# An attention and gated-FFN kernel on one core: halves of matmul pairs dealt as 6, 6 and 12 steps, places planned over the whole loop, one score of long cycles copied by ScalarE

## The chip, the cores and the metric

One Trainium2 chip, one of its cores. A core has TensorE (PE; its weight loads are listed apart as PEld), VectorE (DVE), ScalarE (ACT), GpSimd (POOL) and SyncE (SP, which here issues all DMAs). Each engine runs its own instructions in order and they meet through semaphores. PSUM has eight banks of 128 x 512 fp32 values; TensorE writes them, VectorE and ScalarE read them. The metric is the device time of one execution in microseconds (us).

## The reference: what is computed

```python
# x: 2048 tokens of width 512, all fp32
xn = layernorm(x)
# 32 heads of width 16, all tokens attend to all tokens
q, k, v = split_heads(xn @ wqkv)
p = softmax(q @ k.T * 16**-0.5)
s = merge_heads(p @ v) @ wo
# bilinear gated FFN, width 1792
f = ((xn @ w_gate) * (xn @ w_up)) @ w_down
out = x + s * silu(f)
```

## The kernel before, in words

**Units, rounds, blocks, cycles.** Heads are taken four at a time (8 groups) and queries 512 at a time (4 chunks): 32 units. A unit has 16 rounds, one for each tile of 128 keys; a round has four *positions*, one for each head. So there are 2048 positions. Position q does two things. `expo` computes t, the scores of 128 keys by 512 queries, on TensorE (line 668), and e = exp(t) on ScalarE (line 670) from one of three PSUM banks ("st"). `score` computes, 86 positions ahead of its use (`LEAD`), the scores s of 128 queries by 512 keys (line 646); VectorE reduces them to their maximum (line 648) from one of three other banks ("s"). The maxima of a unit are joined in `maxima`, go through DRAM, and come back as two extra rows of the queries, so that t arrives with the maximum subtracted. t and s of a position use different halves of TensorE's rows and run side by side.

Two rounds, eight positions, make a *block*: `block` multiplies their e with V (pv, line 685; 16 records), into a bank of "st". ScalarE copies the result out (line 698, into one of two single `part` tiles) and GpSimd adds it to the unit's sum. The loop has 256 *cycles*, one for each block: some positions, then the block's pv.

**Filler.** Between the positions of a cycle stand *steps* of other matmuls: the projections of q and k, then the FFN's gate, up and down products, then the output projection. Every fp32 product is made as three products of split operands (high and low part) with 64 rows each, so two sums, a *pair*, run at once on the two halves of TensorE's rows. A pair is made in two halves, because each sum has to pass over both row halves; `pair` (line 283) swaps them in the middle. At the swap a tiny ScalarE activation called `look` (line 304) reads one value of the pair, and the second half's first matmul waits for it. A half has 12 steps, or 15 in the down products of the first two thirds of the FFN. When a pair is done, ScalarE copies one sum and VectorE deals with the other: a copy (line 337), a product (line 387) or an addition (line 462), queued in `before_values` and issued after the cycle's last position, in front of pv.

**What sets the order.** The program's order on TensorE, ScalarE, VectorE and GpSimd is the order in which Python issues it. Three choices set it.

- How many cycles a pair gets, and how its steps fall on them: `spread` and `Filler.fetch`. 240 cycles are shared out in proportion to steps; a pair gets two, three or four. With an odd number, the middle cycle holds the end of the first half and the beginning of the second.
- How many positions a cycle gets: `fits`, seven to nine by its steps, held between one and four positions (`AHEAD`) beyond what the cycle's block needs.
- Where steps stand within a cycle: `Filler.spread` and `Filler.part`, evenly over the gaps between positions; none stands before the second position or after the last but one.

```python
fits = min(9, max(7, int(2.6 + 0.62 * work))) if q + LEAD < TOTAL and work else 8
```

In words below, (p,w) is a cycle of p positions and w steps; (7,4+3) has the swap inside.

**Before the loop.** `early` normalizes the tokens, projects the first keys, queries and all of V, and computes the first 86 scores; a table, `EARLY`, says at which of 265 steps how many scores stand. Each chunk of 512 keys goes through DRAM (`KD`) before scores can use it. **After the FFN**, `ending` projects the output, over the last cycles and beyond the loop.

Of the kernel before, what the change touches and what calls it, by code (L numbers as in the profile page):

```python
# [13 lines left out]
AF = mybir.ActivationFunctionType  # L14
# [16 lines left out]
THIRDS = [range(0, 5), range(5, 10), range(10, 14)]  # L31
LEAD = 86
CYCLES = 240
AHEAD = range(1, 5)
SLOTS = 24 * (NC * (NG // 2 - 1) + 1) + 36 * NF * NC
SPLIT_ROUNDS = 3
EBUFS = 11
HBUFS = 2
QBUFS = 2
EARLY = {66: 4, 75: 4, 84: 4, 93: 4, 104: 4, 113: 4, 124: 6, 137: 4, 144: 2, 150: 2, 156: 4, 162: 2, 166: 2,  # L40
         170: 2, 175: 2, 180: 4, 186: 2, **{n + m: k for n in (192, 216, 240) for m, k in ((0, 2), (6, 2), (12, 4), (18, 2))}}
EARLY_BUFS = {"s": 4, "x": 2, "f": 2}
BUFS = {"st": 3, "s": 3, "misc": 2}
LOWER, UPPER = slice(0, 64), slice(64, P)
BEHIND = mybir.DependencyInfo(mybir.DependencyClass.Sync, mybir.DependencyReason.DATA)
ORDER = mybir.DependencyInfo(mybir.DependencyClass.NoSync, mybir.DependencyReason.SCHED_ONLY)
ORDERED = {mybir.EngineType.PE, mybir.EngineType.Activation, mybir.EngineType.DVE, mybir.EngineType.Pool}


def body(ctx, tc, x, wqkv, wo, wg, wu, wd, out):  # L50
# [87 lines left out]
        while waiting and waiting[0][0] <= steps[0]:  # L138
            waiting.pop(0)[1]()

    before_values, behind_values, lighter = [], [], [False]

    def run_all(queue):
        while queue:
# [489 lines left out]
            for pr in range(2):  # L634
                dma(k[b:b + 2, pr].bitcast(F32), ones)

    def score(n, other, tag="s"):

        i, r = divmod(n, 4 * NT)
        r, j = divmod(r, 4)  # L640
        j ^= other
        kc, t = divmod(r, 4)
        b, pr = 64 * (j % 2), j // 2
        k = ks[(i // NC) % 2]
        o = psum(tag, f"s{i}_{r}_{j}")
        nc.tensor.matmul(o, QS[i][b:b + KB, pr, t * P:(t + 1) * P],  # L646
                         k[b:b + KB, pr, kc * 512:(kc + 1) * 512], start=True, stop=True)
        nc.vector.tensor_reduce(MX[i][:, j, t, kc:kc + 1], o, axis=AX.X, op=OP.max)  # L648

    def maxima(i):  # L650
        mm = keep.tile([P, 3, 4, 4], F32R, name="mm", bufs=2)
# [99 lines left out]
    def early():  # L751
# [76 lines left out]
        def v(*tts):  # L828
            for tt in tts:
                yield from v_proj(wv, tt, "f")  # L830

        at = {n: [] for n in range(265)}
        for c, stats, apply, turns in ((1, (0, 2, 4, 6), (25, 25, 25, 25), (38, 42, 46, 50)),
                                       (2, (26, 26, 28, 30), (60, 60, 73, 75), (70, 74, 79, 83)),
# [4 lines left out]
        for tts, n, root, scale in ((tuple(range(4, 8)), 0, 13, 16), (tuple(range(8, NT)), 16, 52, 53)):  # L839
# [4 lines left out]
        at[150].append((exp_table, None))  # L844
        at[205].append((ahead, 1))
        at[130] += [(ones_columns, slice(8, NT)), (other_keys, None)]
        gens = [k(0), q(0), v(0, 1, 2), k(1), q(1), v(3), k(2), v(4, 5), k(3),
                *[v_pair(wv, (tt, tt + 1), "xf"[tt // 2 % 2]) for tt in range(6, NT, 2)]]
        scored = 0
        stream = (n for g in gens for n in g if n == 1)  # L850
# [45 lines left out]
    class Filler:  # L896
# [4 lines left out]
            self.left, self.queue, self.done = 0, [], False  # L901
            self.plan = []

        def share(self, n, gaps):

            return [n * (i + 1) // gaps - n * i // gaps for i in range(gaps)][::-1]
# [26 lines left out]
        def spread(self, gaps):  # L933
            if isinstance(self.now, tuple):
                a, b = self.now
                self.plan = self.share(a, 2) + [0] + self.share(b, gaps - 3)
            else:
                self.plan = self.share(self.now, gaps)

        def part(self):  # L940
            n = self.plan.pop(0) if self.plan else 0
# [4 lines left out]
                if not self.left:  # L946
                    self.fetch()

    cum = [0]

    def spread(n):
        a = cum[0]
        cum[0] += n
        return max(1, round(cum[0] * CYCLES / SLOTS) - round(a * CYCLES / SLOTS))

    def values(rounds, done):
        if before_values:
            run_all(before_values)
        elif not done:
            step_small(heads)  # L960
        run_all(reduced)
        block(rounds)
        run_all(behind_values)
        if rounds[-1][1] == NT - 1:
            heads.append(finish(rounds[0][0]))
            step_small(heads)
# [9 lines left out]
        lighter[0] = False  # L976
        return True

    def position(q):
# [12 lines left out]
        if j == 3 and kt % 4 == 2:  # L992
            gates.append(lambda: step_small(later))
        ready[n][2].append(expo(i, kt, j))
        scored = q + LEAD
        if scored < TOTAL:
            score(scored, 1)
# [7 lines left out]

    with tc.manual_schedule(engines=ORDERED):
        with banks_of(EARLY_BUFS):
            fil = Filler(filler(early()), spread)
        ctx.enter_context(banks_of(BUFS))
        q = 0  # L1010
        for b in range(NU * NT // 2):
            if fil.done:
                parts = iter([3, 2, 2, 2, 2, 2, 2, 2])
                fil = Filler(ending(), lambda n: next(parts))
# [56 lines left out]
```

## Time and profile before

| | |
|---|---|
| median of 3 runs | 1701.24 us (1701.0 to 1701.58) |
| the profiled execution | 1701.59 us |
| its span, first to last instruction | 1699.8 us |
| granted TensorE clock, mean | 0.999 |
| busy: PE, PEld | 1690.4 us (99%), 1042.1 us (61%) |
| busy: DVE, ACT, POOL | 1436.6 us (85%), 1308.2 us (77%), 875.9 us (52%) |
| DMA | 145.94 MB, mean 86 GB/s |

In rows of groups stand line, engine, operation, the tiles written and read (out<-in), shape, count, then busy us, mean ns of one, idle time before them and what ended it. In rows of the timeline stand start and length in us, engine, line, operation, tiles, shape, count, and in brackets the idle time before the row with what ended it. The end of a matmul is modelled, so its start is the better mark. Rows of the chain of waits have start, length and name.

### The profile page before, as it was taken

To read this page: it belongs to the slowest core of one execution; us is meant where nothing else is said; L and a number is where in the kernel's file an instruction comes from. 1 tells how busy PE (TensorE), PEld (TensorE's weight loads), DVE (VectorE), ACT (ScalarE), POOL (GpSimd) and SP (SyncE) were. 2 spreads that over 40 slices of the span, in tenths; PEclk is the share of its full clock that TensorE was granted. 3 is DMA by queue.
4 is the path that set the end of the run, shared out by engine and by line. 5 is a ranking of instruction groups with operands and counts; after the bars stand their busy time and mean duration, and the time that the engine had idled before them with its cause. 6 is when DMAs were issued, how large, how long until landed. Compare 5 with 4: busy or idle time off the path is not lost.

```text
span 1699.8 us, 35273 instructions
## 1 busy us (share of the span) xinstructions
PE 1690.4 (99%) x13702; PEld 1042.1 (61%) x13702; DVE 1436.6 (85%) x2485; ACT 1308.2 (77%) x2573; POOL 875.9 (52%) x877
## 2 busy tenths in 40 slices
PE   9999999999999999999999999999999999999998
PEld 6766566666565666655656665656666566665665
DVE  7888888888888898888888888888888888898952
ACT  6368777778777788777877887877778777787774
POOL 5125545753645648456354672663647536455661
PEclk9999999999999999999999999999999999999999
DMA  6218623520241312412115220330225112111362
GB/s 228 80 60 251 222 110 128 139 61 29 61 86 41 116 42 79 79 48 62 29 53 133 72 68 23 87 77 27 59 81 127 55 36 65 35 48 47 114 187 90
DMA packets 117507, 145.94 MB, mean 86 GB/s; under 512 B 12700, under 2 KB 74396, under 8 KB 114652
## 3 DMA queue, kind: packets, MB, share of 16 engines
q1 hardware_dynamic: 117340, 143.69, 29.2%
q8 instruction: 108, 1.77, 0.4%
q14 instruction: 59, 0.48, 0.1%
HBM read 95.94 MB, written 47.45 MB: 84 GB/s over the span
## 4 chain that ended last, share of the span: by engine, by line
PE 97%; issue 1%; DMA 1%; POOL 0%; ACT 0%; DVE 0%; SPq 0%; DVEq 0%; ACTq 0%; POOLq 0%
PE pv L685 27%; PE t L668 19%; PE s L646 12%; PE y L296 6%; PE u L296 5%; PE g L296 5%; PE g L300 4%; PE u L300 4%; PE y L300 4%; PE p L296 3%; PE z L296 2%; PE p L300 2%; PE last L685 1%; PE v L300 1%; PE v L296 1%
## 5 line engine op out<-in xcount | busy, mean ns | idle before, releaser
L648 DVE TENSOR_REDUCE mx<-s 128x1 f32<-128x512 f32 x2048 | 1256.6, 683 | 206.6 <-PE s L646 166.2
L670 ACT ACTIVATE e<-t 128x512 f32<-128x512 f32 x2048 | 1099.8, 601 | 94.0 <-PE pv L685 40.0
L668 PE MATMUL t<-qs,ks 50*128 50x512 f32 x2048 | 782.9, 407 | 0.0
L646 PE MATMUL s<-ks,qs 48*128 48x512 f32 x2048 | 769.4, 408 | 0.7 <-DMA ks<-KD 0.5
L64 POOL TENSOR_TENSOR acc<-acc,part 128x512 f32<-128x512 f32 x214 | 280.1, 1309 | 556.7 <-ACT part L698 556.5
L668 PEld LDWEIGHTS t<-qs,ks 50*128 50x128 f32 x2048 | 359.3, 185 | 266.7 <-issue 109.8
L685 PE MATMUL pv<-e,V 128*32 128x512 f32 x3968 | 477.1, 598 | 0.0
L646 PEld LDWEIGHTS s<-ks,qs 48*128 48x128 f32 x2048 | 353.2, 185 | 25.9 <-issue 2.8
L698 ACT ACTIVATE part<-pv 128x512 f32<-128x512 f32 x214 | 128.1, 599 | 204.7 <-PE pv L685 202.3
L685 PEld LDWEIGHTS pv<-e,V 128*32 128x32 f32 x3968 | 103.6, 109 | 234.8 <-issue 214.6
L300 PE MATMUL g<-fh,w1h 64*128 64x512 f32 x224 | 90.5, 404 | 0.0
L296 PE MATMUL u<-fh,w0h 64*128 64x512 f32 x224 | 90.4, 404 | 0.0
L296 PE MATMUL y<-dh,hh 64*128 64x512 f32 x224 | 89.1, 398 | 0.0
L300 PE MATMUL y<-dh,hh 64*128 64x512 f32 x224 | 89.0, 398 | 0.0
L300 PE MATMUL u<-fh,w0l 64*128 64x512 f32 x224 | 88.2, 394 | 0.0
L300 PE MATMUL g<-fl,w1h 64*128 64x512 f32 x224 | 88.1, 393 | 0.0
L300 PE MATMUL g<-fh,w1l 64*128 64x512 f32 x224 | 88.0, 393 | 0.0
L296 PE MATMUL g<-fl,w1h 64*128 64x512 f32 x224 | 88.0, 393 | 0.0
L296 PE MATMUL u<-fh,w0l 64*128 64x512 f32 x224 | 88.0, 393 | 0.0
L296 PE MATMUL g<-fh,w1h 64*128 64x512 f32 x224 | 87.9, 392 | 0.0
L300 PE MATMUL u<-fl,w0h 64*128 64x512 f32 x224 | 87.8, 392 | 0.0
L300 PE MATMUL y<-dh,hl 64*128 64x512 f32 x224 | 87.8, 392 | 0.0
(295 smaller groups left out, 3063.7 us busy)
## 6 DMA issues: line engine op xcount, KB each, us to landing
w1r<-in_wg_dram SPq DMA_DIRECT2D x56, 256.0 KB
w0r<-in_wu_dram SPq DMA_DIRECT2D x56, 256.0 KB
wdr<-in_wd_dram SPq DMA_DIRECT2D x56, 256.0 KB
qs<-QD SPq DMA_DIRECT2D x64, 192.0 KB
ks<-KD SPq DMA_DIRECT2D x12, 768.0 KB
KD<-hl SPq DMA_DIRECT2D x16, 512.0 KB
QD<-hl SPq DMA_DIRECT2D x16, 512.0 KB
OD<-acc SPq DMA_DIRECT2D x31, 256.0 KB
```

Source lines behind the costliest of these rows:

```text
L64: got = getattr(self.engine, name)(*args, **kw)
L296: nc.tensor.matmul(outs[k], l[LOWER], r[LOWER], start=k == 0 and n == 0, stop=(stop or k == 0) and n == len(low) - 1, skip_group_check=k == 1)
L300: nc.tensor.matmul(outs[1 - k], l[UPPER], r[UPPER], start=k == 0 and m == 0, stop=(stop or k == 0) and m == len(high) - 1, skip_group_chec ...
L646: nc.tensor.matmul(o, QS[i][b:b + KB, pr, t * P:(t + 1) * P], k[b:b + KB, pr, kc * 512:(kc + 1) * 512], start=True, stop=True)
L648: nc.vector.tensor_reduce(MX[i][:, j, t, kc:kc + 1], o, axis=AX.X, op=OP.max)
L668: nc.tensor.matmul(o, k[b:b + KR, pr, kt * P:(kt + 1) * P], QS[i][b:b + KR, pr], start=True, stop=True)
L670: nc.scalar.activation(e, o, AF.Exp, scale=DH ** -0.5)
L685: nc.tensor.matmul(o[32 * j:32 * j + 32, c], V[:, kt, h0:h0 + 32], es[j][:, c], start=(kt if whole else n) == 0, stop=kt == NT - 1 if whol ...
L698: nc.scalar.activation(part, o, AF.Copy)
```

## The change

Five things, in the order of the diff.

1. *Dealing of pairs.* Every pair, whatever its steps, counts alike in the sharing of the 240 cycles: of 93 pairs 54 get three cycles and 39 two. The first half of a pair with three cycles is spread over two of them and the second half has the third: 6, 6, 12 steps, or 8, 7, 15. No cycle holds a swap.
2. *Places.* A function `plan` chooses the number of positions of every cycle ahead of the loop, by dynamic programming over how many positions stand ahead (now 0 to 4), with a cost for each cycle from two straight lines (`wait`). It gives 6 positions to cycles of 6 steps, mostly 9 or 10 to those of 12, and 12 to eleven of them. In the last cycles none stands ahead.
3. *A copied score.* In cycles of over 10 steps, from the 29th on, where the plan's formula has it cheaper, the score of one position (the seventh in cycles of 12 steps) is copied by ScalarE into a `part` tile, and VectorE reduces the copy later, when the cycle's last position is issued and the pairs' results are dealt with (`held`). 25 cycles have it.
4. *The first cycle* has 12 positions as before, with 6 steps in place of 12 and none in its first gap.
5. *Before the loop*, the projection of the fourth chunk of keys moves eight steps ahead, in between the steps of a V tile, and `EARLY` asks for some scores a few steps later, two of them at step 262 in place of steps 137 and 144.

```diff
-AHEAD = range(1, 5)
-SLOTS = 24 * (NC * (NG // 2 - 1) + 1) + 36 * NF * NC
+HALVES = [3 * ND] * (NC * (NG // 2 - 1) + 1) + NC * [3 * n for third in THIRDS for n in [ND] * len(third) + [len(third)] * 2]
+PROJECTIONS = 2 * (NC * (NG // 2 - 1) + 1)
+LAST = [3, 2, 2, 2, 2, 2, 2, 2]
+AHEAD = range(0, 5)
...
-EARLY = {66: 4, 75: 4, 84: 4, 93: 4, 104: 4, 113: 4, 124: 6, 137: 4, 144: 2, 150: 2, 156: 4, 162: 2, 166: 2,
-         170: 2, 175: 2, 180: 4, 186: 2, **{n + m: k for n in (192, 216, 240) for m, k in ((0, 2), (6, 2), (12, 4), (18, 2))}}
+EARLY = {66: 4, 75: 4, 84: 4, 93: 4, 104: 4, 113: 4, 124: 6, 144: 4, 150: 2, 156: 4, 162: 2, 167: 2, 172: 2, 176: 2,
+         180: 4, 186: 2, 262: 2, **{n + m: k for n in (192, 216, 240) for m, k in ((0, 2), (6, 2), (12, 4), (18, 2))}}
...
+def cycles_of(k):
+    if k >= len(HALVES):
+        return LAST[k - len(HALVES)]
+    a, b = [round(m * CYCLES / len(HALVES)) for m in (k, k + 1)]
+    return max(1, b - a)
+
+def shares(n, gaps):
+    return [n * (i + 1) // gaps - n * i // gaps for i in range(gaps)][::-1]
+
+def parts_of(n, cycles):
+    if cycles == 1:
+        return [(n, n)]
+    return shares(n, (cycles + 1) // 2) + shares(n, cycles // 2)
+
+def room(work):
+    return 2.36 + 0.603 * work
+
+def wait(places, work, copied):
+    slow = 0.3775 * (places - room(work))
+    full = 0.2575 * places - 0.2275 * work - 0.22
+    return max(0, slow, full), max(0, slow - 0.6, full + 0.4) if copied and work > 10 else 9
+
+def plan():
+    work = [sum(w) if isinstance(w, tuple) else w
+            for k, n in enumerate(HALVES + [3 * ND] * len(LAST)) for w in parts_of(n, cycles_of(k))]
+    states, blocks = {AHEAD[-1]: (0, [8 + AHEAD[-1]])}, NG * NC * NT // 2
+    for b in range(1, blocks - 1):
+        new = {}
+        for ahead, (cost, places) in states.items():
+            for later in AHEAD:
+                n = 8 + later - ahead
+                c = cost + 0.003 * (n - 8) ** 2
+                if 8 * b + LEAD < NG * NC * NT * 4:
+                    c += min(wait(n, work[b], b > PROJECTIONS + 1)) + 0.001 * (n - room(work[b])) ** 2
+                if later not in new or c < new[later][0]:
+                    new[later] = c, places + [n]
+        states = new
+    ahead, (_, places) = min(states.items(), key=lambda s: s[1][0])
+    return places + [8 - ahead]
...
-    def score(n, other, tag="s"):
+    def score(n, other, tag="s", copied=False):
...
-        nc.vector.tensor_reduce(MX[i][:, j, t, kc:kc + 1], o, axis=AX.X, op=OP.max)
+        if copied:
+            kept = part_tile()
+            nc.scalar.activation(kept, o, AF.Copy)
+            held.append(lambda: nc.vector.tensor_reduce(MX[i][:, j, t, kc:kc + 1], kept, axis=AX.X, op=OP.max))
+        else:
+            nc.vector.tensor_reduce(MX[i][:, j, t, kc:kc + 1], o, axis=AX.X, op=OP.max)
...
-        gens = [k(0), q(0), v(0, 1, 2), k(1), q(1), v(3), k(2), v(4, 5), k(3),
+        gens = [k(0), q(0), v(0, 1, 2), k(1), q(1), v(3), k(2), v(4), *between(v(5), 4, k(3)),
...
-                    self.whole, odd = divmod(self.cycles(2 * n), 2)
-                    self.split = max(2, round(n / (2 * self.whole + 1))) if odd else 0
-                    self.more = max(2, self.split - 1) if odd and self.whole else n if odd else 0
-                    self.queue = self.share(n - self.split, self.whole) if self.whole else []
-                    if odd:
-                        self.queue.append((self.split, self.more))
-                    if self.whole:
-                        self.queue += self.share(n - self.more, self.whole)
+                    self.queue = parts_of(n, self.cycles())
...
         elif not done:
             step_small(heads)
+        run_all(held)
         run_all(reduced)
...
-            if b >= NU * NT // 2 - 2:
-                last = TOTAL - 4 * (NU * NT // 2 - 1 - b)
-            else:
-                fits = min(9, max(7, int(2.6 + 0.62 * work))) if q + LEAD < TOTAL and work else 8
-                need = 8 * (b + 1)
-                last = min(max(q + fits, need + AHEAD[0]), need + AHEAD[-1], TOTAL - 4) if b else need + AHEAD[-1]
-            count = last - q
             fil.spread(max(2, count - 2))
...
+            elif b == 0:
+                fil.plan = [0] + shares(work, count - 3)
+            plain, copied = wait(count, work, b > PROJECTIONS + 1 and q + LEAD < TOTAL)
+            unit = (q + count + LEAD) // (4 * NT) > (q + LEAD) // (4 * NT)
+            kept = int(room(work)) - 3 if copied < plain and not unit else -1
             for k in range(count):
...
-                position(q)
+                position(q, k == kept)
```

More of the change, by code (lines that the diff above doesn't have):

```diff
@@ L139, in step @@
             waiting.pop(0)[1]()
-    before_values, behind_values, lighter = [], [], [False]
+    before_values, behind_values, held, lighter = [], [], [], [False]
     def run_all(queue):
@@ L830, in v, with between @@
                 yield from v_proj(wv, tt, "f")
+        def between(outer, n, inner):
+            outer = iter(outer)
+            return [(next(outer) for _ in range(n)), inner, outer]
         at = {n: [] for n in range(265)}
@@ L902, in __init__ @@
             self.plan = []
-        def share(self, n, gaps):
-            return [n * (i + 1) // gaps - n * i // gaps for i in range(gaps)][::-1]
         def fetch(self):
@@ L935, in spread @@
                 a, b = self.now
-                self.plan = self.share(a, 2) + [0] + self.share(b, gaps - 3)
+                self.plan = shares(a, (gaps - 1) // 2) + [0] + shares(b, gaps // 2)
             else:
-                self.plan = self.share(self.now, gaps)
+                self.plan = shares(self.now, gaps)
         def part(self):
@@ L947, in part, with cycles @@
                     self.fetch()
[L949 to L954, printed above, removed]
+    pairs = [0]
+    def cycles():
+        pairs[0] += 1
+        return cycles_of(pairs[0] - 1)
     def values(rounds, done):
@@ L977, in two_finished, with position @@
         return True
-    def position(q):
+    def position(q, copied):
         n, j = divmod(q, 4)
@@ L996, in position @@
         if scored < TOTAL:
-            score(scored, 1)
+            score(scored, 1, copied=copied)
         step()
@@ L1007, in body @@
         with banks_of(EARLY_BUFS):
-            fil = Filler(filler(early()), spread)
+            fil = Filler(filler(early()), cycles)
         ctx.enter_context(banks_of(BUFS))
         q = 0
-        for b in range(NU * NT // 2):
+        for b, count in enumerate(plan()):
             if fil.done:
-                parts = iter([3, 2, 2, 2, 2, 2, 2, 2])
-                fil = Filler(ending(), lambda n: next(parts))
+                fil = Filler(ending(), cycles)
             work = fil.begin()
-            if b >= NU * NT // 2 - 2:
-                last = TOTAL - 4 * (NU * NT // 2 - 1 - b)
-            else:
-                fits = min(9, max(7, int(2.6 + 0.62 * work))) if q + LEAD < TOTAL and work else 8
-                need = 8 * (b + 1)
-                last = min(max(q + fits, need + AHEAD[0]), need + AHEAD[-1], TOTAL - 4) if b else need + AHEAD[-1]
-            count = last - q
             fil.spread(max(2, count - 2))
```

## The prediction

> **What bounds the kernel now.** I read the page first, then the chain of waits in order of time, then single engines' timelines.
>
> ```profile
> span 1699.8 us, 35273 instructions
> PE 97%; issue 1%; DMA 1%; POOL 0%; ACT 0%; DVE 0%; SPq 0%; DVEq 0%; ACTq 0%; POOLq 0%
> L670 ACT ACTIVATE e<-t 128x512 f32<-128x512 f32 x2048 | 1099.8, 601 | 94.0 <-PE pv L685 40.0
> ```
>
> TensorE carries 97% of the chain; other engines show in it only where they make TensorE pause. So I take the loop cycle by cycle: from one block of value products (pv, 16 records) to the next. In the chain each block is a row: start, length, name.
>
> ```profile
> 493.98 1.85 PE pv L685 x16
> 500.07 1.85 PE pv L685 x16
> ...
> 849.86 1.85 PE pv L685 x16
> 855.43 1.86 PE pv L685 x16
> 860.99 1.85 PE pv L685 x16
> 867.04 1.85 PE pv L685 x16
> 874.01 1.85 PE pv L685 x16
> ...
> 1005.22 1.85 PE pv L685 x16
> 1011.95 1.85 PE pv L685 x16
> ...
> 1035.15 1.86 PE pv L685 x16
> 1041.15 0.98 PE pv L685 x5
> ```
>
> I write (p,w) for a cycle of p positions and w steps. The cycles from 849.86 on are (7,8), (7,4+3), (8,9) and (9,12): 5.57, 5.56, 6.05 and 6.97 us. (9,12) has 6 slots (positions and steps together) more than (7,8) and takes 1.40 us more: 0.233 a slot. TensorE alone thus needs 2.07 + 0.233(p+w): 6.73 for (8,12), which the cycle at 1005.22 has, and 6.03 for (8,9). Two kinds exceed it. (7,4+3), where a pair changes halves inside the cycle, should take 5.33 and loses 0.23. (8,7), at 1035.15, should take 5.57, takes 6.00 and loses 0.43. The other kind with a change inside, (8,5+4) at 493.98, takes 6.09 against 6.03 and loses about 0.05.
>
> The first loss is a wait for ScalarE. Three rows of the tile "look" (who waited for it: us, times), then TensorE, ScalarE and a weight load in the cycle at 855.43:
>
> ```profile
>   PEld u L296: 5.8, 25
>   PEld y L296: 3.8, 17
>   PEld p L296: 1.4, 6
> ...
> 859.21 0.40 PE L668 MATMUL t<-qs,ks 50*128 50x512 f32 x1
> 859.35 0.14 ACT L304 ACTIVATE look<-u 1x1 f32<-1x1 f32 x1
> 859.55 0.18 PEld L296 LDWEIGHTS u<-fh,w0h 64*128 64x128 f32 x1 [0.23 <-ACT look L304]
> 859.89 0.40 PE L296 MATMUL u<-fl,w0h 64*128 64x512 f32 x1
> ```
>
> The second half's first step starts 0.34 behind t instead of 0.233, and the next 0.34 behind that: 0.21 in all. Where the halves part at a cycle's end, as in (9,12), nothing is lost.
>
> The second loss is VectorE's pace. Two rows of the cycle at 1035.15 and one of ScalarE from 860.61:
>
> ```profile
> 1037.50 4.28 DVE L648 TENSOR_REDUCE mx<-s 128x1 f32<-128x512 f32 x7 [1.27 <-PE s L646]
> 1037.66 3.53 ACT L670 ACTIVATE e<-t 128x512 f32<-128x512 f32 x7
> ...
> 860.61 1.08 ACT L670 ACTIVATE e<-t 128x512 f32<-128x512 f32 x2
> ```
>
> Reductions run end to end, 4.28/7 = 0.61 each, and with three score banks a score waits for the reduction three before it. A position more costs VectorE 0.61 and TensorE 0.233, difference 0.38; a step more lengthens TensorE's side alone by 0.233. From (8,7), the wait is 0.43 + 0.38(p-8) - 0.233(w-7), nothing where negative. It gives nothing for (9,12) and (7,8), as seen.
>
> **The change part by part.** The counts are the two dealing rules and the planner's rule worked through.
>
> *Waits removed.* Before, 36 pairs hold 8, 4+3 and 9 steps, 13 pairs of fifteens hold 10, 5+4 and 11, and three pairs hold 8, 7, 8, 7. Afterwards every change of halves falls on a cycle's end. Saved: 36 x 0.23 = 8.3; 13 x 0.05 = 0.7; three (8,7), 1.3; three (7,7), 0.05 each by the formula, 0.2; and 0.02 (6.05 against 6.03) in 36 (8,9), 0.7: together 11.2 us.
>
> *New cycles.* Between the first cycle and the end come 87 (6,6), 9 (6,7), 10 (7,8), 73 (9,12), 25 (10,12), 22 with 15 steps, 11 (12,12), 2 (7,6) and two single ones. By the formula (6,6) has -0.10, so no wait, with only 0.10 in hand; (6,7), (7,8), (9,12) and the fifteens none; (10,12) 0.03; (7,6) 0.28, twice: 0.6; (12,12) without a copy 0.79, twice: 1.6.
>
> *The copied score.* It stands in 16 (10,12) and 9 (12,12). One reduction of 0.61 leaves the run that TensorE waits for and comes after the last position, in front of the 1.27 in which VectorE was idle; that idle time hides it, and without it the next cycle's scores would be 0.61 late. So 0.18 of the 0.79 is left on that side. ScalarE gets a copy for it. No row shows one from a score bank; the nearest is the exponential, 0.601 long, two in 1.08, so 0.48 apart, and I take that. The first exponential starts 2.51 behind pv (1037.66 against 1035.15); with the copy among them the ninth starts 9 x 0.48 later, at 6.83, and ends at 7.43. The twelfth t, due at 7.33 (7.66, less 0.33 from the last position to pv), needs its bank, and pv the tenth's, 0.48 later: some 0.1 to 0.2 late each. I take 0.34 a cycle, 9 x 0.34 = 3.1, with 0.18 and 0.79 (the copy frees nothing) as bounds. In (10,12) pv needs the eighth's bank, at 6.95 for a start at 7.20; the copy waits for its score, though, which comes late there, and I take 0.08: with the nine uncopied 1.6 (bounds 0 and 25 x 0.15, some two copies' lateness). Sum of new waits: 0.6 + 1.6 + 3.1 + 1.6 = 6.9.
>
> The Trainium skill has a rule that speaks against the copy: "ScalarE: Activation LUTs", section "What ACT_TABLE_LOAD costs", gives an ACTIVATE with immediate scale 186 ns and 0.833 ns an element, less about 93 ns of overlap back to back, an estimate of 0.52 apart for 512. The trace has 0.48. By the Trainium skill's spacing the nine cycles would pay some 0.5 each more, and the sum below would come out 4.5 higher.
>
> *No position ahead.* Before, each block of pv had at least one position of the next block ahead of it. Afterwards 54 loop cycles, all of 6 or 7 steps, and the whole end have none, so pv's second round needs the exponential just issued. At the kernel's end the parts are seen singly:
>
> ```profile
> 1682.22 0.19 PEld L668 LDWEIGHTS t<-qs,ks 50*128 50x128 f32 x2 [0.84 <-ACT e L670]
> 1682.76 2.07 ACT L670 ACTIVATE e<-t 128x512 f32<-128x512 f32 x4 [0.65 <-PE t L668]
> 1685.31 0.39 PE L296 MATMUL z<-fh,w0l 64*128 64x512 f32 x1
> 1685.68 0.16 PEld L685 LDWEIGHTS last<-e,V 128*32 128x32 f32 x8 [0.35 <-issue]
> 1686.56 0.56 PEld L685 LDWEIGHTS last<-e,V 128*32 128x32 f32 x12 [0.30 <-issue]
> ```
>
> The second round starts 0.88 behind the first. An exponential starts 0.54 behind its t and lasts 0.60; the t stands about 0.35 ahead of pv; so it ends 0.79 into pv, hidden with 0.09 in hand. In these cycles the look (0.14, its row above) can stand ahead of it. I take 0.01 each, 0.5; bounds 0 and 54 x 0.14 = 7.6. Behind it on ScalarE stand pv's part copy and the next exponentials, which begin only when pv has ended.
>
> *The start.* Two places ahead of the loop stall:
>
> ```profile
> 47.44 0.73 PE L646 MATMUL s<-ks,qs 48*128 48x512 f32 x4
> 48.10 0.50 PE L276 MATMUL v<-e,xh 128*128 128x512 f32 x1
> ...
> 55.39 0.72 PE L646 MATMUL s<-ks,qs 48*128 48x512 f32 x3
> 56.37 0.46 PE L646 MATMUL s<-ks,qs 48*128 48x512 f32 x1 [0.26 <-DMA ks<-KD]
> 56.76 0.50 PE L276 MATMUL p<-xh,w1l 128*128 128x512 f32 x1
> ...
> 67.34 0.39 PE L300 MATMUL v<-e,xh 64*128 64x512 f32 x1
> 67.90 0.47 PE L646 MATMUL s<-ks,qs 48*128 48x512 f32 x1 [0.18 <-DVE mx L648]
> 68.59 0.47 PE L646 MATMUL s<-ks,qs 48*128 48x512 f32 x1 [0.22 <-DMA ks<-KD]
> 68.91 0.39 PE L300 MATMUL v<-e,xh 64*128 64x512 f32 x1
> ...
> 90.90 3.68 DVE L648 TENSOR_REDUCE mx<-s 128x1 f32<-128x512 f32 x6 [0.30 <-PE s L646]
> 95.17 7.27 DVE L648 TENSOR_REDUCE mx<-s 128x1 f32<-128x512 f32 x12
> ```
>
> Four scores usually take 0.66 (47.44 to 48.10) and took 1.37 from 55.39 on: 0.71 lost to keys not landed. From 67.34 two slots (0.47) took 1.57: 1.10 lost, to the fourth keys and to VectorE. The change asks for those keys later and makes the fourth eight steps sooner, its store and loads on SP's queue with it: of 1.81 I take 1.5 (bounds 0 and 1.8). But two scores move to just ahead of the loop, where VectorE runs without a break from 90.90 to the first pv: 2 x 0.61 = 1.2 later (bounds 0 and 1.2). In the first cycle, paced by VectorE, six steps that it hid move to cycles paced by TensorE: 6 x 0.233 = 1.4.
>
> *The end.* Four positions move from the loop (4 x 0.233 = 0.9 saved) behind the last steps. There the fourth's exponential starts 0.54 + 3 x 0.48 behind the first t, ends 0.60 later, at 2.58, and the second round (half of 1.86) ends at 3.5; now pv, 1.85 long from 1685.68, ends 2.0 behind that point (1685.31 and a slot: 1685.54). So 1.5 - 0.9 = 0.6 (bounds 0 and 1.5).
>
> The sum: -11.2 + 6.9 + 0.5 - 1.5 + 1.2 + 1.4 + 0.6 = -2.1. The profiled execution took 1701.59, 1.8 of it outside its span, and gives 1699.5; the median of the runs shown, 1701.24, is 0.35 lower: 1699.1.
>
> **The rivals.** *The long cycles cost almost nothing.* Every copied (12,12) at 0.18, (10,12) at 0, no late exponential, the start's 1.8 whole: new waits 1.6 + 1.6 + 0.6 = 3.8, and -11.2 + 3.8 - 1.8 + 1.2 + 1.4 + 0.6 = -6.0: 1695.2. For it: the (9,12) rows show none of either wait. Against: ScalarE's count above. *The last exponential ends too late.* At 0.14 in 54 cycles the 0.5 becomes 7.6: +5.0, 1706.2, slower. It decides from about 0.11 a cycle on. For it: 0.09 in hand is less than one look. Against: where VectorE paces, t comes later but pv does too. *The copy frees nothing.* ScalarE, with one operation more, is late by what VectorE gained, and the nine copied (12,12) pay the 0.79: 9 x 0.45 = 4.1 more, 1703.2. The rule on ScalarE's spacing above points this way; the 0.48 points against it. *The look still waits.* The change moves it and doesn't remove it. If the first step of a second half still paid 0.21 in the 54 pairs of three cycles, 11.3 more: 1710.4. That the token itself must stay, the Trainium skill says: "PSUM — Partial Sum Buffer", section "PSUM bank collisions raise a hardware error", has it that row tiles mustn't use one bank at once and that software must order them. Against it: the (9,12) rows.
>
> **How the numbers follow.** The forecast has 0.45, cheap long cycles 0.30, the late exponential 0.14, the copy that frees nothing 0.08, the look 0.03. 0.2% is 3.4 us, about what a measurement of this kernel can tell from no change: faster is below 1697.8, slower above 1704.6. Faster gets the 0.30 and 0.10 of the forecast's lower side; slower gets 0.03 and 0.11 of the late exponential; the rest is the same. The range goes from below the cheap rival to just under the late exponential, 1693.5 to 1705.
>
> **What would show it.** The waits for look in the loop fall from 48 to a few, and (6,6) cycles take 4.87 with pv blocks 4.87 apart. (12,12) cycles take 8.0, (10,12) 7.2 to 7.3. The first pv stands within 0.5 of where it stood. If pv waits for an exponential in the cycles of 6 steps, or they take over 4.95, the forecast is wrong upward; if (12,12) takes 7.7 to 7.85, downward.

## The result and the profile after

The changed kernel takes 1710.24 us (median of 6 runs, 1709.19 to 1710.58); the kernel before, in the same rounds, 1701.38 (1701.0 to 1701.94). The ratio is 1.0052, 95% interval 1.0042 to 1.0063: slower by 8.9 us, where 2.1 us less was forecast, and above the range that ended at 1705. The profiled execution took 1710.56.

From the page of the changed kernel: the span and the chain by engines.

```profile
span 1708.5 us, 35368 instructions
PE 91%; POOL 3%; DMA 2%; DVE 2%; issue 1%; ACT 1%; SPq 0%; DVEq 0%; POOLq 0%; ACTq 0%
```

TensorE's share of the chain fell from 97% to 91%, and GpSimd and DMA, which had 0% and 1%, now carry 3% and 2%: parts of the chain that run past TensorE. The ordinary cycles come out as forecast. These are block starts in the chain of waits of the changed kernel:

```profile
896.15 1.85 PE pv L744 x16
904.23 1.92 PE pv L744 x16
909.16 1.85 PE pv L744 x16
914.01 1.85 PE pv L744 x16
920.97 1.85 PE pv L744 x16
927.91 1.85 PE pv L744 x16
935.12 1.93 PE pv L744 x16
```

A copied (12,12) takes 8.08, the second (6,6) after it 4.85, two (9,12) 6.96 and 6.94, a (10,12) 7.21. (In the chain the block that ends a long cycle stands some 0.07 early, with a row of 1.92 or 1.93 instead of 1.85; from pv's first record to the next the (12,12) takes 8.14 and the (6,6) behind it 4.87.) So I took every cycle of both traces from the first record of one pv to that of the next, and subtracted 2.07 + 0.233(p+w), with 1.40/6 for 0.233. A wait inside a pv thus counts in the cycle behind it. Cycles are numbered from 0 here: cycle 0 is the first, and the 243rd pv ends cycle 242. What is left, in us:

| | before | after |
|---|---|---|
| start of the span to first pv | 101.12 | 100.46 |
| first pv to 243rd pv | 1507.49 | 1514.72 |
| of it waits, by that formula | 9.4 | 15.7 |
| 243rd pv to the end | 91.2 | 93.3 |
| waits by kind, before | (7,4+3) and (7,7) 7.7, (8,7) 1.2, (8,9) and (8,5+4) 0.9 | |
| waits by kind, after | | (12,12) 6.8, (9,12) 5.9, (10,12) 1.5, (6,6) 1.3, (7,6) 0.6, (8,12) 0.4 |

The kinds of after don't lie evenly. 83 of 87 (6,6) and 68 of 73 (9,12) wait for less than 0.1; the 5.9 sits in five (9,12) cycles, and two of these, cycles 4 and 12, have 1.02 and 3.78. (The others are cycle 20 with 0.69, which waits for a `part` tile, and cycles 92 and 144 with 0.42 and 0.45, whose wait lies in the pv ahead of them.) In cycles 4 and 12 TensorE waits for something that it didn't wait for in the kernel before. Cycle 4, from TensorE's timeline:

```profile
126.14 0.47 PE L700 MATMUL s<-ks,qs 48*128 48x512 f32 x1 [0.56 <-DMA qs<-QD]
```

The first pair has three cycles where it had two, so its query projection is stored a cycle later (on SP's queue from 118.06 on instead of 113.84) and the score stands at a query that hasn't landed. Cycle 12, from the chain of waits:

```profile
150.53 10.01 DMA ks<-KD
160.54 0.02 issue
160.56 7.49 DMA QD<-hl
...
168.85 1.29 POOL hl L118
170.14 0.58 POOL tr L118
170.72 1.23 POOL acc L118
171.96 0.02 issue
171.98 0.61 ACT part L757
172.59 0.04 issue
172.63 0.54 PE t L727
173.17 0.42 PE p L350
173.60 0.42 PE p L350
```

Read from below: t waits because ScalarE copies pv's result only at 171.98, into a `part` tile that GpSimd frees at 170.72 plus 1.23; GpSimd was busy splitting a projection into `hl`, whose two buffers were still being stored to DRAM; and those stores stood on SP's queue behind eight loads of the second group's keys. GpSimd's and TensorE's timelines have the two waits:

```profile
165.81 0.61 POOL L118 CAST hl<-qr 128x512 fp32r<-128x512 f32 x1 [3.96 <-DMA KD<-hl]
```

```profile
172.63 0.54 PE L727 MATMUL t<-qs,ks 50*128 50x512 f32 x1 [1.97 <-ACT part L757]
```

SP's timeline shows the order, in the kernel before and then in the changed kernel:

```profile
144.92 0.97 SPq L64 DMA_DIRECT2D KD<-hl  x2
146.85 1.42 SPq L64 DMA_DIRECT2D QD<-hl  x2
148.32 7.24 SPq L64 DMA_DIRECT2D ks<-KD  x8
```

```profile
147.70 8.58 SPq L118 DMA_DIRECT2D ks<-KD  x8
157.37 1.39 SPq L118 DMA_DIRECT2D KD<-hl  x2
159.36 1.51 SPq L118 DMA_DIRECT2D QD<-hl  x2
```

These stores are the third pair's. The first five pairs end in cycles 1, 4, 6, 9 and 11 in the kernel before and in cycles 2, 4, 7, 9 and 12 in the changed one, so the third pair's projection is split from 147.71 on instead of 142.90, while the loads are asked for at almost the same time. The wait is 1.97, the cycle loses 3.78. The last rows of the chain show the rest: after the pause steps are 0.43 apart instead of 0.233. The last section has the clock.

The end grew too. The last cycle's timeline on ScalarE, TensorE and the weight loads:

```profile
1688.04 1.92 PE L744 MATMUL last<-e,V 128*32 128x512 f32 x16
...
1690.48 2.07 ACT L729 ACTIVATE e<-t 128x512 f32<-128x512 f32 x4 [1.74 <-PE t L727]
...
1693.64 2.06 ACT L729 ACTIVATE e<-t 128x512 f32<-128x512 f32 x4
1694.29 0.50 PE L727 MATMUL t<-qs,ks 50*128 50x512 f32 x1 [0.46 <-ACT e L729]
1694.72 2.09 PE L744 MATMUL last<-e,V 128*32 128x512 f32 x24
```

The last block begins 6.68 after the one before it, against 5.31 (1680.37 to 1685.68) in the kernel before: ScalarE has eight exponentials in this cycle instead of four.

### The profile page after: what moved, and what is told of

It is laid out like the page before. It is cut to its first block, busy times and chain, and to the rows that moved or that the text cites. A ratio compares the mean times of both kernels' runs of the same rounds, so it can differ in the third digit from the quotient of the medians.

```text
span 1708.5 us, 35368 instructions
## 1 busy us (share of the span) xinstructions
PE 1694.5 (99%) x13702; PEld 1059.9 (62%) x13702; DVE 1446.2 (85%) x2479; ACT 1312.6 (77%) x2602; POOL 882.0 (52%) x883
## 4 chain that ended last, share of the span: by engine, by line
PE 91%; POOL 3%; DMA 2%; DVE 2%; issue 1%; ACT 1%; SPq 0%; DVEq 0%; POOLq 0%; ACTq 0%
PE pv L744 25%; PE t L727 18%; PE s L700 11%; PE y L350 5%; PE u L350 5%; PE g L350 5%; PE g L354 4%; PE y L354 4%; PE u L354 4%; PE z L350 2%; PE p L350 2%; PE p L354 1%; DVE mx L707 1%; PE last L744 1%; PE z L354 1%
## 5 line engine op out<-in xcount | busy, mean ns | idle before, releaser
L727 PE MATMUL t<-qs,ks 50*128 50x512 f32 x2048 | 790.9, 408 | 3.4 <-ACT part L757 2.9
L700 PE MATMUL s<-ks,qs 48*128 48x512 f32 x2048 | 784.9, 411 | 1.9 <-DVE mx L707 1.2
L744 PEld LDWEIGHTS pv<-e,V 128*32 128x32 f32 x3968 | 108.6, 109 | 227.9 <-issue 174.1
L350 PE MATMUL g<-fh,w1l 64*128 64x512 f32 x224 | 88.0, 393 | 0.0
L354 PE MATMUL g<-fl,w1h 64*128 64x512 f32 x224 | 87.9, 393 | 0.0
L354 PE MATMUL g<-fh,w1l 64*128 64x512 f32 x224 | 87.9, 393 | 0.0
L354 PE MATMUL u<-fh,w0h 64*128 64x512 f32 x224 | 87.9, 393 | 0.0
L350 PE MATMUL u<-fl,w0h 64*128 64x512 f32 x224 | 87.9, 392 | 0.0
L354 PE MATMUL u<-fl,w0h 64*128 64x512 f32 x224 | 87.9, 392 | 0.0
L350 PE MATMUL u<-fh,w0h 64*128 64x512 f32 x224 | 87.9, 392 | 0.0
```

Source lines behind the costliest of these rows:

```text
L350: nc.tensor.matmul(outs[k], l[LOWER], r[LOWER], start=k == 0 and n == 0, stop=(stop or k == 0) and n == len(low) - 1, skip_group_check=k == 1)
L354: nc.tensor.matmul(outs[1 - k], l[UPPER], r[UPPER], start=k == 0 and m == 0, stop=(stop or k == 0) and m == len(high) - 1, skip_group_chec ...
L727: nc.tensor.matmul(o, k[b:b + KR, pr, kt * P:(kt + 1) * P], QS[i][b:b + KR, pr], start=True, stop=True)
L744: nc.tensor.matmul(o[32 * j:32 * j + 32, c], V[:, kt, h0:h0 + 32], es[j][:, c], start=(kt if whole else n) == 0, stop=kt == NT - 1 if whol ...
```

## The experiments

My theory after the two traces: the cycles of the loop are about even, as much lost to VectorE in long cycles as was gained at the swaps, and the 8.9 us come from local accidents (the pile-up at cycle 12, the wait in cycle 4, the end). The rival: the cycles themselves cost more, through the copy or through cycles with no position ahead. The kernel before, measured with each group of runs, had medians of 1700.85, 1700.54 and 1701.17, and 1701.38 in the rounds of the result. They drift by up to 0.8, so what a run gives back is told as its distance from the kernel before of its own rounds, against the changed kernel's 8.9.

### The keys loaded later

```diff
-            if kt == 0 and g + 1 < NG and c == 1:
+            if kt == (6 if g == 0 else 0) and g + 1 < NG and c == 1:
                 load_k(g + 1)
```

> The changed kernel, but the loads of the second group's keys (8 DMAs of 192 KB) are issued six rounds later; nothing else differs. Theory 'pile-up': in the changed kernel these loads stand on SP's queue ahead of a projection's stores, the stores land late, GpSimd's split waits for its hl buffers, the part tile for GpSimd, a bank for the part tile, and TensorE stands still at 170.28 for 2.35 us, after which the clock is low: cycle 12 should fall from 10.75 to about 7.0 us and the total by 3.8, to about 1706.4. Rival 'places': the loss lies in the long cycles and at the end; cycle 12's wait only shifts to a later cycle and the total stays within 1 us of 1710.2.

1707.19, ratio 1.0035 (1.0023 to 1.0048): 6.3 above the kernel before instead of 8.9, so 2.5 are given back (3.05 between the two times themselves). Cycle 12 waits for nothing, and first pv to 243rd pv is 1510.98 in the trace, 3.74 shorter. The pile-up is shown.

### The loads issued earlier, in the kernel before

```diff
-            if kt == 0 and g + 1 < NG and c == 1:
+            if (i, kt) == (0, 13) or kt == 0 and 0 < g < NG - 1 and c == 1:
                 load_k(g + 1)
```

> The kernel before, with only the loads of the second group's keys issued some three rounds earlier, so that they stand ahead of a projection's stores on SP's queue. Theory 'pile-up': the same chain appears, a wait of TensorE for the part tile behind GpSimd around 150 to 175 us, and +2 to +4.5 us: 1703.5 to 1706. Rival: the loads' place does not matter, 1701.4 within 0.6.

1701.0, ratio 1.0001 (0.9992 to 1.0009): no wait, a miss. SP's timeline of this run tells why: the loads went out whole before the projection was split, ahead of the stores by a cycle, not between split and store.

```profile
133.50 4.20 SPq L64 DMA_DIRECT2D ks<-KD  x8
```

```profile
144.62 4.99 SPq L64 DMA_DIRECT2D KD<-hl  x2
149.70 0.95 SPq L64 DMA_DIRECT2D QD<-hl  x2
```

So the loads a cycle ahead of the stores don't hurt here. In the changed kernel, and below with the dealing alone, they stand directly ahead of stores whose buffers are wanted next; this run doesn't make that order, so it neither shows nor refutes the pile-up.

### No copy

```diff
-            kept = int(room(work)) - 3 if copied < plain and not unit else -1
+            kept = -1
```

> The changed kernel without the copied score (every score is reduced by VectorE from its bank). If the copy frees what the prediction took: the nine copied cycles of 12 positions and 12 steps go from 0.47 to 0.7 to 0.8 of wait, 16 cycles of 10 and 12 lose about 0.05 of wait: +1.5 to +2.5, about 1712. Rival 'the copy frees nothing': within 0.5 of 1710.2.

1709.78, ratio 1.0053 (1.004 to 1.0066): the copy is worth nothing in sum, the number of the rival. Its mechanism is not the rival's: by kind the copy does what it is for: without it (12,12) has a median wait of 0.71 instead of 0.47 and 9.1 us together instead of 6.8. But (10,12) falls from 1.5 to 0.5, and the single waits in cycles 31, 36, 139 and 240 (0.35, 0.89, 0.21, 0.36) are gone. The copied score takes one of the `part` tiles that pv's result needs; in the first three of these cycles ScalarE's copy of that result waits until VectorE has reduced the copied score, and in cycle 240 a score waits for a reduction that stands behind it. ScalarE in cycle 36 of the changed kernel:

```profile
325.12 0.60 ACT L757 ACTIVATE part<-pv 128x512 f32<-128x512 f32 x1 [0.94 <-DVE mx L705]
```

The 0.89 is not steady: with the copy cycle 36 loses 0.22 in one of the other runs and 1.26 in another. Cycle 12, ahead of the first copy, loses 1.77 in this trace instead of 3.78, which is not the copy's doing. Without that cycle the loop's waits are 11.8 with the copy and 11.9 without.

### Four positions left for the end

```diff
-    ahead, (_, places) = min(states.items(), key=lambda s: s[1][0])
-    return places + [8 - ahead]
+    return states[AHEAD[-1]][1] + [8 - AHEAD[-1]]
```

> The changed kernel, with four positions ahead at the end of the loop in place of none (the planner's last state is set to 4), as the kernel before had. The stretch from the 243rd block of value products to the end took 93.3 us in the changed kernel and 91.2 before; theory: it goes back to about 91.3, four positions are paid in the loop (0.9), so -1.2 in all, about 1709.0. Rival: the end costs nothing by itself, 1710.2.

1708.01, ratio 1.0041 (1.0028 to 1.0055): 7.2 above the kernel before, so 1.7 are given back. From the 243rd pv to the end it takes 91.1, as before the change; cycle 12 still loses 4.1.

### The dealing alone, in the kernel before

```diff
-                    self.whole, odd = divmod(self.cycles(2 * n), 2)
...
-                        self.queue += self.share(n - self.more, self.whole)
+                    c = self.cycles(2 * n)
+                    self.queue = [(n, n)] if c == 1 else self.share(n, (c + 1) // 2) + self.share(n, c // 2)
...
-        return max(1, round(cum[0] * CYCLES / SLOTS) - round(a * CYCLES / SLOTS))
+        cum[1] += 1
+        return max(1, round(cum[1] * CYCLES / 93) - round((cum[1] - 1) * CYCLES / 93))
...
-                fits = min(9, max(7, int(2.6 + 0.62 * work))) if q + LEAD < TOTAL and work else 8
+                fits = min(9, max(6, int(2.6 + 0.62 * work))) if q + LEAD < TOTAL and work else 8
```

(`AHEAD` is `range(0, 5)` here too.)

> The kernel before with the dealing alone: every pair two or three whole cycles, 6, 6 and 12 steps; places by the old rule (as many as fit, 6 to 9, none to four ahead), no copy, the old start. Theory (the swaps' wait is worth what the cycles of before show, and without the plan the positions that the six-step cycles don't hold come back as waits): worked through, the rule gives 43 cycles (7,6), 12 (8,6) and 34 (6,6). The removed waits are 9.4 us; by the formula of the prediction the new ones are 43 x 0.28 + 12 x 0.66 + 1.3 = 21.4; six steps leave the first cycle, 1.4, and the first pair's query store comes later, about 1. So 1701.2 + 13 to 14: 1714 to 1715. Rival (the dealing is the gain and the plan the loss): faster than before, 1692 to 1698.

1719.87, ratio 1.0116 (1.0102 to 1.013). The block starts show a (7,6) and an (8,6):

```profile
485.30 1.85 PE pv L685 x16
490.69 1.85 PE pv L685 x16
496.67 1.85 PE pv L685 x16
```

5.39 and 5.98, so 0.28 and 0.65 to 0.69 lost; 43 and 12 of them make 12.2 and 8.3, each within 0.4 of what was worked out. Cycle 4 loses 1.25, of the 1 expected. Of the 5 us above the expectation 3.35 are cycle 12's, and 0.9 lie behind the 243rd pv. So the pile-up comes with the dealing and not with plan or copy; the loads stand ahead of the stores on SP's queue here too:

```profile
148.45 9.09 SPq L64 DMA_DIRECT2D ks<-KD  x8
158.66 1.13 SPq L64 DMA_DIRECT2D KD<-hl  x2
```

### The start alone, in the kernel before

```diff
-EARLY = {66: 4, 75: 4, 84: 4, 93: 4, 104: 4, 113: 4, 124: 6, 137: 4, 144: 2, 150: 2, 156: 4, 162: 2, 166: 2,
-         170: 2, 175: 2, 180: 4, 186: 2, **{n + m: k for n in (192, 216, 240) for m, k in ((0, 2), (6, 2), (12, 4), (18, 2))}}
+EARLY = {66: 4, 75: 4, 84: 4, 93: 4, 104: 4, 113: 4, 124: 6, 144: 4, 150: 2, 156: 4, 162: 2, 167: 2, 172: 2, 176: 2,
+         180: 4, 186: 2, 262: 2, **{n + m: k for n in (192, 216, 240) for m, k in ((0, 2), (6, 2), (12, 4), (18, 2))}}
...
-        gens = [k(0), q(0), v(0, 1, 2), k(1), q(1), v(3), k(2), v(4, 5), k(3),
+        gens = [k(0), q(0), v(0, 1, 2), k(1), q(1), v(3), k(2), v(4), *between(v(5), 4, k(3)),
```

> The kernel before with the start alone: the fourth keys eight steps sooner and the new table of early scores. In the two traces the first pv came 0.66 us sooner in the changed kernel. Theory: the start is worth that 0.66 and nothing else, 1700.2 to 1700.5. Rival: two scores just ahead of the loop delay something behind the first pv: 1701 to 1702.

1700.12, ratio 0.9997 (0.9988 to 1.0007): no difference that can be told; the first pv comes 0.28 sooner, the time is 0.4 lower.

### The first pair in two cycles

```diff
-    a, b = [round(m * CYCLES / len(HALVES)) for m in (k, k + 1)]
+    a, b = [int(m * CYCLES / len(HALVES)) for m in (k, k + 1)]
```

> The changed kernel with the sharing of cycles rounded down: the first pair has two cycles instead of three (the others shift by one place now and then; 54 threes and 39 twos stay). Theory: the wait of the fifth cycle for the queries' way through DRAM (1.0) goes, and six steps go back into the first cycle, which VectorE paces (1.4): 1707.6 to 1708.4, with the pile-up of loads, stores and splits in the thirteenth cycle either as it was or moved, since the pairs' results now come a cycle sooner (if it goes as well, 1704.5). Rival (the wait is only shifted to another pair): 1709.5 to 1710.5.

1705.21, ratio 1.0028 (1.0017 to 1.0039): 4.7 above the kernel before, so 4.2 of the 8.9 are given back, the case in which the pile-up goes as well. Neither cycle 4 nor cycle 12 waits, and SP's timeline has the stores in front again:

```profile
144.28 0.91 SPq L118 DMA_DIRECT2D KD<-hl  x2
146.21 1.26 SPq L118 DMA_DIRECT2D QD<-hl  x2
147.52 6.66 SPq L118 DMA_DIRECT2D ks<-KD  x8
```

One line of rounding carries about half of the loss, but it moves more than one pair. The whole pattern of threes and twos is shifted by a place, 78 of the 93 pairs have another number of cycles, and the first five end in cycles 1, 4, 6, 9 and 11, as in the kernel before. So cycle 4 is freed by the first pair's earlier end, and cycle 12 by the third's.

### The gates' operations two positions sooner

```diff
-                if k == count - 1:
+                if k == max(1, count - 3):
                     run_all(gates)
+                if k == count - 1:
                     done = two_finished(q)
```

> The changed kernel with the gates' small operations issued ahead of the last but two position of a cycle instead of ahead of its last. Theory: in the cycles at 669.5, 995.0, 1283.8 and 1608.0 us pv's second round waits some 0.42 for the last exponential, which stands behind a gate's tanh on ScalarE while no position is ahead; with the tanh two positions sooner all four go: 1710.2 - 1.7 = 1708.5. Rival (no position ahead is what costs, the tanh only happens to stand there): 1710.

1710.7, ratio 1.0055 (1.0043 to 1.0068): no gain, a miss. What it was to remove was real. ScalarE in the changed kernel at the pv that ends cycle 91, a (6,6) with no position ahead, and that pv (begun at 669.53) in the chain of waits:

```profile
669.64 0.14 ACT L358 ACTIVATE look<-u 1x1 f32<-1x1 f32 x1
669.69 0.61 ACT L447 ACTIVATE e<-y 128x512 f32<-128x512 f32 x1
670.21 0.57 ACT L729 ACTIVATE e<-t 128x512 f32<-128x512 f32 x1
```

```profile
669.60 2.28 PE pv L744 x15
```

A gate's operation of 0.61 stands ahead of the exponential that pv's second round needs, and this pv takes 2.28 instead of 1.85. The pvs of cycles 91, 143, 189 and 241 lost 0.34 to 0.45 by it, counted in the cycles behind them. With the operation sooner those cycles behind lose at most 0.12 by it, but now cycles 91, 143, 189 and 241 themselves lose 0.24 to 0.30, since it delays other exponentials; in the waits of this run stands a line that the changed kernel doesn't have (waited for: us, times, longest):

```profile
PE pv L744 <- ACT e L729: 2.2, 7, 0.5
```

The wait moved, which is the rival's reading: with no position ahead, the half microsecond that ScalarE spends near the end of these four cycles is paid either way.

### All local causes removed

The edits of "the keys loaded later", "four positions left for the end", "the first pair in two cycles" and "the gates' operations two positions sooner" together, and this one:

```diff
-            kept = int(room(work)) - 3 if copied < plain and not unit else -1
+            kept = int(room(work)) - 3 if copied < plain and not unit and count > 11 and "pairs" in fst else -1
```

> The changed kernel with every local cause that the traces name taken away: the keys of the second group loaded six rounds later (3.0 by the run before), four positions left ahead for the end (2.2), the first pair in two cycles (1.0 to 2.4), the gates' small operations two positions sooner, off the last exponential's way (4 cycles x 0.42 = 1.7), and the copy only in cycles of 12 positions once both part tiles exist (about 1). Theory (the loss is a sum of separate accidents around a trade that is even): 1710.2 - 3.0 - 2.2 - 2 - 1.7 - 1 = 1700.3, level with the kernel before. Rival (six-step cycles with no position ahead cost something everywhere): 1704 or more.

1702.27, ratio 1.0012 (1.0003 to 1.0021). Against the kernel before of the same rounds, 1.7 is left of 8.9; the waits in the loop are 10.9 against 9.4. That lies between the theory's 1700.3 and the rival's 1704: the dealing with its accidents taken away is a shade slower than the kernel before, by 0.12%. Largest single wait left: in the (12,12) that begins at 289.4, 0.88 for a `part` tile.

### Another plan, four and five positions ahead

The kernel of the last run without the copy, with the prediction's formula as the plan's cost; the last two lines of the diff, one position more ahead, are the second run's alone.

```diff
 def wait(places, work, copied):
-    slow = 0.3775 * (places - room(work))
-    full = 0.2575 * places - 0.2275 * work - 0.22
-    return max(0, slow, full), max(0, slow - 0.6, full + 0.4) if copied and work > 10 else 9
+    return max(0, 0.43 + 0.38 * (places - 8) - 0.233 * (work - 7)), 9
...
-AHEAD = range(0, 5)
+AHEAD = range(0, 6)
```

> The kernel with all local causes removed, without the copy, and with the plan's cost of a cycle replaced by the prediction's wait formula (four ahead at most, as before). Worked through, it takes no cycle of 12 positions and 12 steps: 24 (7,6), 40 (10,12), 70 (6,6). Theory (a six-step cycle's positions must go somewhere, and wherever they go VectorE asks about the same): 24 x 0.28 + 40 x 0.06 + 0.5 = 9.6 of waits in place of the 10.9 there: 1701 to 1701.5, level with the kernel before. Rival (the long cycles were the whole loss): 1697 or less.

1702.39, ratio 1.0008 (0.9999 to 1.0017). There is no (12,12) in it, 24 (7,6) wait 7.6 and 40 (10,12) 2.2, together with the rest 10.9: the same sum as with eleven (12,12). That is the theory's reading, a microsecond above its number.

> The same with up to five positions ahead: 13 (7,6), 44 (10,12), 81 (6,6), 9 where a cycle has fewer steps; 13 x 0.28 + 44 x 0.06 + 0.3 = 6.6 of waits: 1698 if five ahead cost nothing. Rival: eleven e tiles hold a block and three more, so the fourth and fifth exponential ahead wait for pv's first round, and ScalarE starts the next cycle with a backlog; at 0.2 in some 60 cycles, 1710.

1713.21, ratio 1.0071 (1.0058 to 1.0085): the rival, and at a higher price in fewer places. In 20 cycles a t just behind pv waits for a bank that a late exponential still reads, a line of the waits that the run with four ahead doesn't have; and ScalarE's timeline in one of these cycles shows why it is late:

```profile
PE t L724 <- ACT e L726: 7.2, 20, 0.4
```

```profile
416.34 0.60 ACT L726 ACTIVATE e<-t 128x512 f32<-128x512 f32 x1 [1.55 <-PE pv L741]
```

ScalarE sits idle for 1.55 ahead of the last exponential, until pv, begun at 415.26, has read a first e tile and so freed it. This cycle loses 0.62. A kernel with more e tiles wasn't tried.

## Why the prediction was wrong, point by point

**What bounds the kernel** was right, and so was the formula. VectorE's pace, 0.43 + 0.38(p-8) - 0.233(w-7), gave 0.28 for (7,6), 0.28 measured; 0.66 for (8,6), a mean of 0.69 measured with the dealing alone; no wait for (6,6) with 0.10 in hand, and 83 of 87 have none; 0.79 for an uncopied (12,12), where the run without the copy has a median of 0.71.

**Waits removed**, -11.2. The cycles of before held 9.8 of it: (7,4+3) and (7,7) 7.7 of 8.5, (8,7) 1.2 of 1.3, (8,5+4) and (8,9) 0.9 of 1.4. The single cycle from which I took 0.23 was a little worse than the mean of 0.20 over 39, and I took 0.02 and 0.05 from distances of block starts that scatter by as much. Mis-sized by 1.4. No second half waits for its look in the loop of after, so the rival of the look that still waits is out. That its 1710.4 lies within 0.2 of the measured time is luck.

**New cycles and the copied score**, +6.9. (7,6), (10,12) and (12,12) came to 8.9: 0.6 as forecast, 1.5 against 1.6, and 6.8 against 4.7. A copied (12,12) waits 0.47, not 0.34, midway between my bounds; the run without the copy shows that it saves 0.24 of 0.71. The sum is high also because one cycle without a copy, cycle 141, loses 1.6, and 1.56 in the run without any copy: there a score waits for a reduction that stands on VectorE behind a transposition, `acc<-tr`, which itself waits 1.47 for GpSimd. That the copy holds a `part` tile until VectorE comes to it, and with it some 1.8 us in cycles 31, 36, 139 and 240, I had not seen: I followed the copy on VectorE and ScalarE and not the buffer that it writes. My spacing of 0.48 for ScalarE doesn't decide it. By the Trainium skill's figure of 0.52 for an ACTIVATE back to back ("ScalarE: Activation LUTs", "What ACT_TABLE_LOAD costs") the nine would have paid 0.5 more each, and they paid 0.13 more; the last cycles have four in 2.07, so 0.49 apart, not 0.52.

**No position ahead**, +0.5. The rival of the late exponential as I told it (54 x 0.14) is out, but its mechanism showed in four of the 54, the (6,6) that are cycles 91, 143, 189 and 241: pv waited for the last exponential, which I had named as a sign that the forecast is too low. They paid some 0.4 each, 1.6 in all instead of 0.5, behind a gate's operation of 0.61 that I had not listed among what can stand ahead of that exponential. The table has the 1.6 in the cycles behind them.

**"Between the first cycle and the end ... (9,12) ... none"** is the step that failed. As a rule for kinds it held; in cycles 4 and 12 it missed 4.8, and the single waits in cycles 20, 31, 36, 139 and 240, for a `part` tile or behind the copy's reduction, add 2.5. I had priced the first pair's third cycle only as six steps moved, +1.4, and did not ask which stores, loads and splits come a cycle later when the first and the third pair end a cycle later. The first pair's query store came too late for cycle 4; the third pair's stores fell behind the loads of the second group's keys on SP's queue, and that stalled cycle 12. The run with the pattern shifted gave 4.2 back, the one with the keys later 2.5.

**The start**, -0.3: the first pv came 0.66 sooner in the changed kernel; alone the start brings 0.3. **The end**, 1.5 less the 0.9 saved in the loop: behind the 243rd pv it was 2.1. My 1.5 for the last block was near its 1.4; missing was that the twelve cycles before it, with nothing ahead, take 1.1 longer together (72.86 against 71.76); what follows the last block is 0.4 shorter. The trace of the run with four left is 2.2 shorter in all, 0.7 of it because cycle 36's wait happens to be shorter there.

Summed up in one trace each, the 11 us between -2.1 and the profiled +9.0: 1.4 too much removed; 2.0 too little for the three kinds; 7.3 of single waits not foreseen (4.8 in cycles 4 and 12, 2.5 for `part` tiles and the copy's reductions); 0.8 too little for no position ahead (1.3 that doesn't already stand in a (12,12), against 0.5); 0.6 at the end and 0.4 for positions and steps moved too little; 0.4 at the start in the other direction; 0.3 outside the span. That is 12.4; the 1.3 over are the many cycles that lie some hundredths below the line that I subtract.

## What to carry to other kernels

When a piece of work takes one cycle longer, follow not only its steps but all that its end sets off, each store, load and buffer release, and look at which queue entries they now stand behind; a formula for the ordinary case says nothing about the one place where two bursts meet. Moving work between cycles under a fixed total mostly moves the wait: positions that six-step cycles can't hold came back at the same price whichever cycles took them. And a copy to relieve one engine takes a buffer from whoever shares it.

## What the runs showed of the hardware that was not expected

A short pause of TensorE can cost nearly its length again. Windows of the changed kernel around cycle 12, then one of the run without the copy (window, its length, then busy us and instructions of PE, PEld, DVE, ACT and POOL, the granted clock, DMA share, GB/s):

```profile
171.95:172.95 1.00, 0.32 (x2) 0.30 (x4) 0.69 (x2) 0.97 (x2) 0.30 (x1) 1.00 1.07 418
172.95:176.37 3.42, 3.42 (x18) 2.66 (x16) 1.95 (x3) 2.29 (x5) 1.00 (x1) 0.50 1.07 352
```

```profile
173.33:176.74 3.41, 3.41 (x34) 2.62 (x34) 3.39 (x6) 3.17 (x7) 0.44 (x1) 1.00 1.07 354
```

After the wait of 1.97, from 172.95 to 176.37, the clock is granted at 0.50: 18 matmul records where the other run has 34 in as long a stretch. Half of 3.42 is 1.7, which is where nearly all of the other 1.8 of the 3.78 went. After a wait of 1.49 in the same place, in the run without the copy, the clock stays at 1.00, and that cycle lost 1.8 in all. The runs with waits of 1.55 (the dealing alone), 1.67 (gates sooner) and 2.24 (four for the end) in the same place have such a stretch at 0.50 of 3.41 to 3.42 us too; those with 0.88 to 1.0 elsewhere do not. The Trainium skill ("TensorE: Matmul & The Clock Gate", Part 1) tells of such a gate at half the clock, released after some 3.4 us of work, and agrees with the length. It asks for an idle window of about 3.4 us before the clock falls; here 1.55 was enough and 1.49 was not.

Where the wait fell doesn't tell these five runs apart. In every trace the granted clock stays at 1.00 for a whole number of stretches of 3.413 us. In the four runs in which it falls inside the loop, it does so after 49 of them (from 5.70 to 172.95 in the changed kernel), and in the 49th TensorE sat idle for 1.97, 1.55, 1.67 and 2.17 us. The run without the copy has its 1.49 inside the 49th as well. So the length of the wait is what differs, with the limit between 1.49 and 1.55 of 3.41 us as far as five traces can tell.
